# Attention with relative bias, then a leaky-ReLU FFN: one FFN piece fewer per head pair, and the next pair's q and k turned and copied in the pair's first half

## The chip, the cores and the metric

One core of a Trainium2 chip runs the whole program. The metric is the device time of one execution in microseconds (us), median over runs.

## The reference, cut to what matters

```python
# q, k, v: (8, 8, 576, 64), bias_table: (32, 8)
scores = q @ k.T / 8 + bias            # bias depends on the distance of the positions and the head
attn = exp(scores - max); attn /= sum(attn)
x = (attn @ v) as (4608 tokens, 512)   # 8 heads of 64 side by side
h = x @ w_in                           # 512 -> 2048
out = maximum(0.01 * h, h) @ w_out     # 2048 -> 512, float32
```

## The kernel before, in words

The attention goes by pairs of heads: `items` lists 8 batches of 4 pairs, so pair n runs from 0 to 31. The FFN goes by tiles of 512 tokens, nine of them. The engines' orders are the program's own: `manual_schedule` (line 68) keeps on each engine the order in which the code issues, and every engine works its queue in order. What stands where is therefore set by the loop at lines 553 to 596 alone.

For a pair, `qk_mm` (line 296) makes the transposed scores: u = 0 to 3 are the four blocks of 128 keys against queries 0 to 511 (line 311, PSUM tile `ps_s`, two buffers), u = 4 holds the same keys against the last 64 queries (line 304, tile `ps_q`), u = 5 the last 64 keys (lines 314 and 315). `exp` (line 321) takes the exponentials on ScalarE into `at`, and `band` (line 332) multiplies the band around the diagonal with the exponentiated bias on VectorE (line 346). One pair later `av_tails` and `av` (lines 350 and 363) make the value products: a first half for the pair's first head, 20 matmuls at line 370 that VectorE divides at lines 373 and 374 (`rcp`, `opair`), and a second half for the other head. Both halves live in one PSUM tile `ps_o`, which has a single buffer of two banks (tag "o"), and the `ps_q` of the running pair takes the same buffer. `x_transposes` turns the result into `xT`, by TensorE for the first pairs (line 392, copied at line 393) and by a DMA transpose from pair 6 on.

q and k are needed with the head dimension on partitions. `pair_rows` (line 249) packs them (`pr`, line 254), and they are turned on TensorE for pairs 0 to 9 (line 275, six transposes for q and six for k), and by a DMA transpose into `tu` three pairs ahead from pair 10 on (line 262). `transpose_q` and `transpose_k` (lines 286 and 291) then copy them on VectorE into `qt` and `kt`, and line 281 makes a masked copy of the last 64 keys.

The FFN is cut into pieces of four matmuls of 512 columns. An in-piece (line 415, then the leaky ReLU on ScalarE, line 417) makes one block of 128 of the 2048 inner features; four out-pieces (line 426) make 128 tokens of the result, copied on VectorE into `y` (line 431) and stored by SP. Both use the PSUM tag "m" with two buffers. `moe(n)` issues up to n in-pieces, `moe_block` four pieces, two and two, out-pieces if a tile is ready for that and in-pieces otherwise. After pair 31, `moe_rest` issues what is left and may use all PSUM.

In a steady pair before, the queue of TensorE is: scores 0 and 1, tails, first half of the value products of the pair before, in-piece, second half, in-piece, scores 2, 3 and 4, two out-pieces, score 5, two out-pieces, two in-pieces. The copies into `qt` and `kt` for the next pair stand on VectorE behind the last band product and ahead of the copy into `y`. For pairs 5 to 9 (issued in pairs 4 to 8) the twelve transposes stand between score 5 and the second half of the block, both in one "o" tile `ps_tt`.

Of the kernel before, what the change touches and what calls it, by code (L numbers as in the profile page):

```python
# [11 lines left out]
BF16 = mybir.dt.bfloat16  # L12
# [25 lines left out]
def kernel(  # L38
# [17 lines left out]
    P = 128  # L56
    n_pairs = H // 2
# [21 lines left out]
    ps_o_pool = ctx.enter_context(tc.tile_pool(name="ps_o", bufs=1, space=bass.MemoryType.PSUM))  # L79
    ps_m_pool = ctx.enter_context(tc.tile_pool(name="ps_m", bufs=2, space=bass.MemoryType.PSUM))  # L80
# [163 lines left out]
    N = len(items)  # L244
    AHEAD = 3

    prs, turned = {}, {}
# [9 lines left out]
    def by_dma(n):  # L257
        return n >= 2 * n_pairs + 2
# [5 lines left out]
    def turned_pair(n, j):  # L264

        if by_dma(n):
            return turned[n][:, j * NC : (j + 1) * NC, :].rearrange("p c r -> p r c")
        if n <= n_pairs:
            ps = ps_m_pool.tile([P, 8 * P], BF16, name="ps_t", tag="m")
        else:  # L270
            if j == 0:
                turned[n] = ps_o_pool.tile([P, 2, 8 * P], BF16, name="ps_tt", tag="o")
            ps = turned[n][:, j, :]
        for c in range(NC):
            nc.tensor.transpose(ps[:, c * RQ : (c + 1) * RQ], in_=prs[n][0:RQ, j, c, :],
                                identity=ident[0:RQ, 0:RQ])
        return ps[:, 0:S].rearrange("p (c r) -> p r c", c=NC)

    def apart(t):

        nc.vector.tensor_tensor(
            out=t[:, S : S + P].rearrange("p (e i) -> p e i", e=2),
            in0=t[:, NJ * P : S].unsqueeze(1).to_broadcast([P, 2, SL]),
            in1=own, op=ALU.mult)

    def transpose_q(n):
        qt = qts[n] = qt_pool.tile([P, S], BF16, name="qt")
        copy = nc.scalar.copy if n <= n_pairs and n != 1 else nc.vector.tensor_copy
        copy(out=qt[:, 0:S].rearrange("p (r c) -> p r c", c=NC), in_=turned_pair(n, 0))  # L289

    def transpose_k(n):
        kt = kts[n] = kts_[n % 2]
        nc.vector.tensor_copy(out=kt[:, 0:S].rearrange("p (r c) -> p r c", c=NC), in_=turned_pair(n, 1))  # L293
        apart(kt)

    def qk_mm(n, u):

        qt, kt = qts[n], kts[n]
        if u == NJ:
            ps = ps_o_pool.tile([P, 2, 512], FP32, name="ps_q", tag="o")  # L300
            for c in range(NJ):
                for e in range(2):
                    r = slice(e * D, (e + 1) * D)
                    nc.tensor.matmul(ps[:, e, c * SL : (c + 1) * SL], lhsT=kt[r, c * P : (c + 1) * P],
                                     rhs=qt[r, 512:S], start=True, stop=True)
            return ps
        ps = ps_s_pool.tile([P, 2, 512], FP32, name="ps_s")
        if u < NJ:
            for e in range(2):
                r = slice(e * D, (e + 1) * D)  # L310
                nc.tensor.matmul(ps[:, e, :], lhsT=kt[r, u * P : (u + 1) * P], rhs=qt[r, 0:512],  # L311
                                 start=True, stop=True)
        else:
            nc.tensor.matmul(ps[:, 0, :], lhsT=kt[:, S : S + P], rhs=qt[:, 0:512], start=True, stop=True)
            nc.tensor.matmul(ps[:, 1, 0:SL], lhsT=kt[:, S : S + P], rhs=qt[:, 512:S], start=True, stop=True)  # L315
        return ps
# [4 lines left out]
    def exp(n, u, ps):  # L321
        at, at4 = at_view(n), at4_[n % 2]
        if u < NJ:
            nc.scalar.activation(at[:, :, u, 0:512], ps, AF.Exp, scale=scale)  # L324
        elif u == NJ:
            nc.scalar.activation(at[:, :, :, 512:S],  # L326
                                 ps[:, :, 0 : NJ * SL].rearrange("p e (c i) -> p e c i", i=SL),
                                 AF.Exp, scale=scale)
        else:
            nc.scalar.activation(at4[:, 0:S], ps.rearrange("p e i -> p (e i)")[:, 0:S], AF.Exp, scale=scale)  # L330
# [19 lines left out]
    def av_tails(n):  # L350

        b, p = items[n]
        at4 = at4_[n % 2]
        ops_[n] = op_pool.tile([P, NJ + 1, 2 * D], BF16, name="opair")
        ps = outs[n] = ps_o_pool.tile([P, 2, 512], FP32, name="ps_o", tag="o")
        for ic in range(NJ + 1):
            for e in range(2):
                r = slice(e * SL, (e + 1) * SL)
                nc.tensor.matmul(ps[:, e, ic * (D + 1) : (ic + 1) * (D + 1)],  # L359
                                 lhsT=at4[r, ic * P : (ic + 1) * P], rhs=v4[b % NBUF][r, p, :],  # L360
                                 start=(ic == 0), stop=False)
# [15 lines left out]
    def x_by_dma(n):  # L377
        return n_pairs + 2 <= n < N - 1
# [61 lines left out]
    def can(kind):  # L440
        T = made[kind]
        if running[kind] is not None:
            return True
        if kind == "in":
            return T < made["ready"] and T < made["out"] + 2
        return T < made["in"]

    def piece(kind):

        nonlocal share  # L450
        if running[kind] is None:
            running[kind] = (ffn_in if kind == "in" else ffn_out)(made[kind])
            left[kind] = n_fc
            if kind == "in":
                share = left["out"]
        next(running[kind])
        left[kind] -= 1
        if left[kind] == 0:
            next(running[kind], None)
            running[kind] = None  # L460
            made[kind] += 1
# [8 lines left out]
    def moe(n_pieces):  # L470
        for _ in range(n_pieces):
            if can("in"):
                piece("in")

    def moe_block():

        kind = "out" if can("out") else "in"
        for i in range(4):
            if can(kind):
                piece(kind)  # L480
            if i == 1:
                yield
        yield

    def moe_rest():
        rest["on"] = True
        while (kind := choose()):
            piece(kind)

    def finished(n):  # L490
        b, p = items[n]
        if p == n_pairs - 1:
            while made["ready"] < n_tt and (made["ready"] + 1) * TT <= (b + 1) * S:
                made["ready"] += 1
# [17 lines left out]
    def begin(n):  # L512
        b, p = items[n]
        if n == 0:
            load_w_in(0)
            load_v(1, 0, H, False)
            load_w_in(1)
            load_w_out(0)
            load_w_out(1)
        elif 0 < b < B - 1:  # L520
            if p < 2:
                load_qk(b + 1, 4 * p, 4 * p + 4)
            if p > 0:
                load_v_part(b + 1, p - 1)
        if n + 1 < N and not by_dma(n + 1):
            pair_rows(n + 1)
        if n + AHEAD < N and by_dma(n + AHEAD):
            pair_rows(n + AHEAD)
            turn_by_dma(n + AHEAD)
# [22 lines left out]

    for n in range(2, N + 1):
        live = n < N
        early = n + 1 <= n_pairs
        if x_by_dma(n - 2):
            finished(n - 2)
        if live:
            begin(n)
            ps_a, ps_b = qk_mm(n, 0), qk_mm(n, 1)  # L560
            exp(n, 0, ps_a)
            exp(n, 1, ps_b)
        av_tails(n - 1)
        av(n - 1, 0)
        if live:
            band(n, 0)
        if early:
            transpose_q(n + 1)
        moe(1)
        av(n - 1, 1)  # L570
        if live:
            band(n, 1)
        if early:
            transpose_k(n + 1)
        moe(1)
        if live:
            ps_a, ps_b, ps_c = qk_mm(n, 2), qk_mm(n, 3), qk_mm(n, 4)
            exp(n, 2, ps_a)
            band(n, 2)
            exp(n, 3, ps_b)  # L580
            exp(n, 4, ps_c)
            band(n, 4)
        x_transposes(n - 1)
        if not x_by_dma(n - 1):
            finished(n - 1)
        block = moe_block()
        next(block)
        if live:
            ps_a = qk_mm(n, 5)
            exp(n, 5, ps_a)  # L590
            band(n, 5)
        if n + 1 < N and not early:
            transpose_q(n + 1)
            transpose_k(n + 1)
        next(block)
        moe(2)
    moe_rest()


# [28 lines left out]
```

## Time and profile before

| | |
|---|---|
| median of 3 runs | 429.24 us (428.47 to 433.93) |
| profiled execution | 429.74 us, of which the span of its instructions 428.0 us |
| mean granted clock of TensorE | 0.976 |
| busy share of the span | TensorE 88%, ScalarE 56%, VectorE 47%, GpSimd 16% |

A window row gives start and end in us from the span's start and what each engine was busy in it. A timeline row gives start, duration, engine, line, what was written and read, how many instructions were merged, and in brackets how long the engine had stood idle and what ended it. A line "A <- B: total, times, longest" in the view of waits says that A waited for B. A few matmul records are missing from the trace, so counts of matmuls are a little low.

### The profile page before, as it was taken

How to read it: one execution, taken by the hardware profiler on the slowest of the kernel's cores; microseconds unless marked ns; L12 is line 12 of the kernel's file. 1: busy time of each engine (PE TensorE's matmuls, PEld its weight loads, DVE VectorE, ACT ScalarE, POOL GpSimd, SP SyncE). 2: the span in 40 equal slices, each digit the busy share in tenths (PEclk: the TensorE clock that was granted, in tenths of full speed). 3: DMA queues.
4: the chain of work that ended last, by engine and by line, in shares of the span. 5: the costliest groups of instructions: out<-in, count | busy, mean ns of one | idle time of the engine just before them, and what ended most of it. 6: DMA issues, size and time to landing. Idle time of an engine off the chain costs nothing.

```text
span 428.0 us, 8434 instructions
## 1 busy us (share of the span) xinstructions
PE 376.7 (88%) x3458; PEld 191.6 (45%) x3512; DVE 200.2 (47%) x517; ACT 239.5 (56%) x343; POOL 67.8 (16%) x98
## 2 busy tenths in 40 slices
PE   7777688778995999979999999999999999999995
PEld 2454344444443444444444444444444444444442
DVE  5457444665555555555555555555555520010121
ACT  3728475555686666666666666666666626316000
POOL 8734321015002400330042004000000000000000
PEclk9959899999998999999999999999999999999999
DMA  9999993149822984595479536943411100010111
GB/s 106 190 198 193 205 150 57 47 74 163 145 40 47 174 142 66 84 168 98 69 94 177 101 69 91 101 70 69 69 41 41 41 26 25 26 74 0 51 74 74
DMA packets 103613, 39.90 MB, mean 93 GB/s; under 512 B 82576, under 2 KB 97944, under 8 KB 103576
## 3 DMA queue, kind: packets, MB, share of 16 engines
q0 software_dynamic: 53664, 18.36, 41.9%
q1 hardware_dynamic: 49912, 21.02, 23.8%
q8 instruction: 27, 0.44, 0.4%
q14 instruction: 10, 0.08, 0.1%
HBM read 37.68 MB, written 9.45 MB: 110 GB/s over the span
## 4 chain that ended last, share of the span: by engine, by line
PE 55%; DVE 20%; ACT 15%; issue 7%; DMA 1%; another core or an unknown queue 1%; ACTq 0%; POOL 0%; POOLq 0%
PE pm L415 21%; PE pm L426 15%; PE ps_o L370 11%; ACT at L324 8%; DVE at L346 5%; PE ps_s L311 5%; ACT at L330 3%; DVE opair L374 3%; DVE y L431 3%; DVE qt L289 3%; DVE kt L293 3%; ACT at L326 3%; DVE rcp L373 1%; PE ps_o L359 1%; ACT gt L417 1%
## 5 line engine op out<-in xcount | busy, mean ns | idle before, releaser
L415 PE MATMUL pm<-xT,w_in_sb 128*128 128x512 bf16 x546 | 138.4, 379 | 14.8 <-DVE y L431 9.4
L417 ACT ACTIVATE gt<-pm 128x512 bf16<-128x512 f32 x144 | 86.2, 602 | 114.6 <-PE pm L415 114.5
L324 ACT ACTIVATE at<-ps_s 128x1024 bf16<-128x1024 f32 x128 | 124.0, 1027 | 34.0 <-PE ps_s L311 34.0
L426 PE MATMUL pm<-w_out_sb,gt 128*128 128x512 bf16 x553 | 130.7, 380 | 1.9 <-issue 0.7
L346 DVE TENSOR_TENSOR at<-at,hk 128x768 bf16<-128x768 bf16 (+3 forms) x160 | 72.0, 454 | 66.1 <-ACT at L324 30.5
L415 PEld LDWEIGHTS <-w_in_sb 128*128 128x128 bf16 x576 | 52.5, 98 | 71.4 <-issue 19.3
L426 PEld LDWEIGHTS <-gt 128*128 128x128 bf16 x576 | 53.0, 98 | 61.2 <-issue 1.0
L370 PE MATMUL ps_o<-vn,at 128*128 128x65 bf16 x1280 | 52.6, 198 | 5.5 <-DVE opair L374 5.5
L431 DVE COPY y<-pm 128x512 f32<-128x512 f32 x36 | 24.7, 687 | 69.1 <-PE pm L426 66.1
L370 PEld LDWEIGHTS <-at 128*128 128x128 bf16 x1280 | 47.3, 101 | 16.7 <-issue 11.9
L311 PE MATMUL ps_s<-qt,kt 64*128 64x512 bf16 x256 | 41.4, 396 | 10.3 <-DVE kt L293 7.0
L119 POOL DMA_DIRECT2D vn<-in_v_dram x24 | 21.1, 891 | 173.4 <-PE ps_o L370 168.7
L373 DVE RECIPROCAL rcp<-ps_o 128x5 f32<-128x5 f32 x64 | 12.5, 195 | 73.0 <-PE ps_o L370 72.8
L374 DVE TENSOR_TENSOR opair<-ps_o,rcp 128x320 bf16<-128x320 f32 x64 | 31.5, 491 | 2.2
L311 PEld LDWEIGHTS <-kt 64*128 64x128 bf16 x256 | 8.0, 95 | 36.0 <-issue 26.5
L330 ACT ACTIVATE at<-ps_s 128x576 bf16<-128x576 f32 x32 | 21.8, 681 | 1.7 <-PE ps_s L315 1.6
L326 ACT ACTIVATE at<-ps_q 128x512 bf16<-128x512 f32 x32 | 19.7, 617 | 0.0
L359 PEld LDWEIGHTS <-at 64*128 64x128 bf16 x320 | 9.5, 95 | 11.3 <-DVE at L346 2.5
L293 DVE COPY kt<-tu 128x576 bf16<-128x576 bf16 x22 | 14.3, 651 | 0.0
L289 DVE COPY qt<-tu 128x576 bf16<-128x576 bf16 x22 | 14.2, 647 | 0.0
L111 POOL DMA_DIRECT2D qn<-in_q_dram x17 | 12.0, 706 | 12.7 <-DVE pr L254 10.0
L359 PE MATMUL ps_o<-v,at 64*128 64x65 bf16 x320 | 11.1, 193 | 3.0 <-DVE at L346 1.9
(53 smaller groups left out, 165.7 us busy)
## 6 DMA issues: line engine op xcount, KB each, us to landing
out_dram<-y SPq DMA_DIRECT2D x36, 256.0 KB, 2.2
vn<-in_v_dram POOLq DMA_DIRECT2D x28, 128.0 KB, 5.4
qn<-in_q_dram POOLq DMA_DIRECT2D x12, 288.0 KB, 7.2
kn<-in_k_dram POOLq DMA_DIRECT2D x12, 288.0 KB, 7.9
w_in_sb<-in_moe_w_in_dram POOLq DMA_DIRECT2D x2, 1024.0 KB, 14.8
w_out_sb<-in_moe_w_out_dram POOLq DMA_DIRECT2D x2, 1024.0 KB, 16.0
qn<-in_q_dram POOLq DMA_DIRECT2D x4, 144.0 KB, 4.2
kn<-in_k_dram POOLq DMA_DIRECT2D x4, 144.0 KB, 4.5
```

Of the source, the lines that this page charges most:

```text
L293: nc.vector.tensor_copy(out=kt[:, 0:S].rearrange("p (r c) -> p r c", c=NC), in_=turned_pair(n, 1))
L311: nc.tensor.matmul(ps[:, e, :], lhsT=kt[r, u * P : (u + 1) * P], rhs=qt[r, 0:512], start=True, stop=True)
L324: nc.scalar.activation(at[:, :, u, 0:512], ps, AF.Exp, scale=scale)
L326: nc.scalar.activation(at[:, :, :, 512:S], ps[:, :, 0 : NJ * SL].rearrange("p e (c i) -> p e c i", i=SL), AF.Exp, scale=scale)
L330: nc.scalar.activation(at4[:, 0:S], ps.rearrange("p e i -> p (e i)")[:, 0:S], AF.Exp, scale=scale)
L346: nc.vector.tensor_tensor(out=o, in0=o, in1=m, op=ALU.mult)
L370: nc.tensor.matmul(ps[:, ic, :], lhsT=at[:, o : o + P], rhs=vn[b % NBUF][:, c, 2 * p + e, :], start=False, stop=(ic == NJ and c == NJ - 1))
L374: nc.vector.tensor_tensor(out=opair[:, :, e * D : (e + 1) * D], in0=ps[:, :, 0:D], in1=rcp.to_broadcast([P, NJ + 1, D]), op=ALU.mult)
L415: nc.tensor.matmul(pm, lhsT=w_in_sb[:, c, f * P : (f + 1) * P], rhs=xT[c][:, t0 : t0 + TT], start=(c == 0), stop=(c == n_cc - 1))
L417: nc.scalar.activation(gt[:, f, :], pm, AF.Prelu, bias=0.0, scale=1.0, alpha=0.01)
L426: nc.tensor.matmul(pm, lhsT=gt[:, f, ts * P : (ts + 1) * P], rhs=w_out_sb[:, f, :], start=(f == 0), stop=(f == n_fc - 1))
L431: nc.vector.tensor_copy(out=y, in_=pm)
```

## The change

The transposes and copies for the next pair's q and k move up: q's behind the first half of the value products, k's behind the second, in every pair and not in pairs 2 and 3 alone. The transposes on TensorE that used the "o" buffer now use the "m" buffers, one tile for q and one for k. The last `moe(2)` becomes `moe(1)`, so that a full pair holds 28 FFN matmuls in place of 32.

```diff
@@ turned_pair @@
-        if n <= n_pairs:
-            ps = ps_m_pool.tile([P, 8 * P], BF16, name="ps_t", tag="m")
-        else:
-            if j == 0:
-                turned[n] = ps_o_pool.tile([P, 2, 8 * P], BF16, name="ps_tt", tag="o")
-            ps = turned[n][:, j, :]
+        ps = ps_m_pool.tile([P, 8 * P], BF16, name="ps_t", tag="m")
@@ the loop over pairs @@
-        early = n + 1 <= n_pairs
+        more = n + 1 < N
...
-        if early:
+        if more:
             transpose_q(n + 1)
         moe(1)
         av(n - 1, 1)
         if live:
             band(n, 1)
-        if early:
+        if more:
             transpose_k(n + 1)
         moe(1)
...
-        if n + 1 < N and not early:
-            transpose_q(n + 1)
-            transpose_k(n + 1)
         next(block)
-        moe(2)
+        moe(1)
```

The rules that choose pieces are unchanged, but they meet other numbers. FFN matmuls by pair, counted in the two programs (a full pair is two in-pieces in the first half, four out-pieces, and the rest in-pieces; an in-pair has in-pieces alone; the last row holds what follows pair 31):

| pair | 4 | 5 | 6 | 7, 8 | full pairs | in-pairs | short pairs | 31 | from then on |
|---|---|---|---|---|---|---|---|---|---|
| before | 24 | 32 | 24 | 16 each | 32 in 9, 13 to 15, 17 to 30 | 32 in 10 | 16 in 11, 12, 16 | 32 | 8, then 344 |
| after | 20 | 28 | 16 | 16 each | 28 in 9, 10, 13 to 16, 18 to 25, 27 to 30 | 28 in 11, 17, 26 | 12 in 12 | 28 | 8, then 420 |

On VectorE, in a full pair before (line 373 divides the second head; the `at` rows are the bands 1, 2, 4 and 5; then the copies for the next pair, the copy into `y`, and the packing for a pair further on):

```order
L373 RECIPROCAL rcp<-ps_o 128x5
L374 TENSOR_TENSOR opair<-ps_o,rcp 128x5x64
L346 TENSOR_TENSOR at_113<-at_113,hk 128x2x384 x2
L346 TENSOR_TENSOR at_113<-at_113,hk 128x2x320
L346 TENSOR_TENSOR at_0_115<-at_0_115,hk_101 128x192
L289 COPY qt<-tu 128x576
L293 COPY kt_111<-tu 128x576
L281 TENSOR_TENSOR kt_111<-kt_111,own 128x128
L431 COPY y<-pm_2833 128x512
L254 COPY pr<-qn_103 96x768
```

In a full pair after, from the first division on, the `qt` copy stands between the two divisions, the `kt` copy and its masked part behind band 1, and the copy into `y` has only the bands ahead of it:

```order
L369 TENSOR_TENSOR opair<-ps_o,rcp 128x5x64
L341 TENSOR_TENSOR at_114<-at_114,hk 128x2x256
L284 COPY qt<-tu 128x576
L368 RECIPROCAL rcp<-ps_o 128x5
L369 TENSOR_TENSOR opair<-ps_o,rcp 128x5x64
L341 TENSOR_TENSOR at_114<-at_114,hk 128x2x384
L288 COPY kt_110<-tu 128x576
L276 TENSOR_TENSOR kt_110<-kt_110,own 128x128
L341 TENSOR_TENSOR at_114<-at_114,hk 128x2x384
L341 TENSOR_TENSOR at_114<-at_114,hk 128x2x320
L341 TENSOR_TENSOR at_1_116<-at_1_116,hk_101 128x192
L426 COPY y<-pm_2960 128x512
```

So three copies went from behind band 5 to the first half, and `y` moved up by them.

On ScalarE, two full pairs before: the exponentials (lines 324, 326, 330) and the leaky ReLUs of the in-pieces (line 417), which show where TensorE's in-pieces stand:

```order
L324 ACTIVATE at_113<-ps_s 128x2x512 x2
L417 ACTIVATE gt<-pm_2776 128x512
L417 ACTIVATE gt<-pm_2806 128x512
L324 ACTIVATE at_113<-ps_s 128x2x512 x2
L326 ACTIVATE at_113<-ps_q 128x8x64
L330 ACTIVATE at_0_115<-ps_s 128x576
L417 ACTIVATE gt<-pm_2862 128x512
L417 ACTIVATE gt<-pm_2868 128x512
```

One full pair after, lines 319, 321, 325 and 412 being the same four:

```order
L319 ACTIVATE at_114<-ps_s 128x2x512 x2
L412 ACTIVATE gt<-pm_2901 128x512
L412 ACTIVATE gt<-pm_2933 128x512
L319 ACTIVATE at_114<-ps_s 128x2x512 x2
L321 ACTIVATE at_114<-ps_q 128x8x64
L325 ACTIVATE at_1_116<-ps_s 128x576
L412 ACTIVATE gt<-pm_2985 128x512
```

The second in-piece behind the block is gone from the pair; it is issued later, in the end with the 420.

On VectorE in pair 7, where TensorE does the turning, before: both copies read the one tile `ps_tt` behind band 5.

```order
L346 TENSOR_TENSOR at_1_116<-at_1_116,hk_101 128x192 [waits Activation_49]
L289 COPY qt<-ps_tt 128x576 [waits PE_49]
L293 COPY kt_110<-ps_tt 128x576 [waits PE_49]
L281 TENSOR_TENSOR kt_110<-kt_110,own 128x128 [waits DVE_49]
L431 COPY y<-pm_1253 128x512 [waits PE_49]
```

After, each reads a tile of its own, in the first half:

```order
L369 TENSOR_TENSOR opair<-ps_o,rcp 128x5x64 [waits DVE_49]
L341 TENSOR_TENSOR at_114<-at_114,hk 128x2x256 [waits Activation_49]
L284 COPY qt<-ps_t 128x576 [waits PE_49]
L368 RECIPROCAL rcp<-ps_o 128x5 [waits PE_49]
L369 TENSOR_TENSOR opair<-ps_o,rcp 128x5x64 [waits DVE_49]
L341 TENSOR_TENSOR at_114<-at_114,hk 128x2x384 [waits Activation_49]
L288 COPY kt_110<-ps_t 128x576 [waits PE_49]
```

The transposes that fill these tiles moved with them on TensorE, and k's no longer stand behind q's in one tile.

## Rows read from the trace of the kernel before

**Rows 1.** Waits, whole span: who waited for whom, total us, times, longest

```profile
PE pm L415 <- DVE y L431: 9.4, 18, 0.8
...
PE ps_tt L275 <- DVE qt L289: 7.6, 5, 1.7
PE ps_s L311 <- DVE kt L293: 7.0, 3, 3.2
```

**Rows 2.** Windows: length, then PE, PEld, DVE, ACT, POOL busy, clock, DMA, GB/s

```profile
41.11:56.62 15.51, 11.29 (x120) 6.39 (x120) 7.26 (x20) 8.42 (x13) 4.80 (x6) 0.89 1.36 201
56.62:71.05 14.43, 11.05 (x127) 5.91 (x121) 6.03 (x15) 9.26 (x15) 2.68 (x4) 1.00 1.11 79
71.05:81.61 10.56, 9.14 (x109) 5.04 (x105) 5.73 (x14) 6.00 (x10) 0.00 (x0) 1.00 0.31 48
81.61:91.88 10.27, 7.31 (x97) 4.19 (x96) 6.79 (x18) 5.01 (x6) 0.00 (x0) 1.00 0.48 72
...
113.04:124.00 10.96, 10.09 (x110) 5.14 (x104) 5.36 (x14) 9.16 (x16) 0.00 (x0) 1.00 0.23 46
133.66:143.19 9.53, 7.83 (x85) 4.26 (x84) 5.49 (x15) 5.02 (x6) 6.29 (x9) 0.82 1.15 103
175.43:185.12 9.69, 6.43 (x84) 3.42 (x78) 5.04 (x14) 6.86 (x11) 7.03 (x10) 1.00 1.40 113
206.68:217.36 10.68, 10.08 (x110) 5.06 (x103) 5.95 (x15) 6.98 (x12) 0.00 (x0) 1.00 0.45 70
335.49:349.16 13.67, 13.23 (x157) 7.15 (x152) 5.79 (x15) 8.27 (x13) 0.00 (x0) 1.00 0.12 34
349.16:423.44 74.28, 73.95 (x337) 33.56 (x343) 8.52 (x13) 20.30 (x34) 0.00 (x0) 1.00 0.11 43
```

**Rows 3.** Timeline of TensorE in pair 19, a full pair

```profile
206.08 0.61 PE L311 MATMUL ps_s<-qt,kt 64*128 64x512 bf16 x4
...
210.36 0.28 PE L304 MATMUL ps_q<-qt,kt 64*128 64x64 bf16 x8
...
214.28 1.03 PE L415 MATMUL pm<-xT,w_in_sb 128*128 128x512 bf16 x4
215.80 1.02 PE L415 MATMUL pm<-xT,w_in_sb 128*128 128x512 bf16 x4 [0.49 <-DVE y L431]
216.76 0.60 PE L311 MATMUL ps_s<-qt,kt 64*128 64x512 bf16 x4
```

**Rows 4.** Timeline of VectorE in pair 19

```profile
209.16 0.19 DVE L373 RECIPROCAL rcp<-ps_o 128x5 f32<-128x5 f32 x1 [0.53 <-PE ps_o L370]
209.39 0.49 DVE L374 TENSOR_TENSOR opair<-ps_o,rcp 128x320 bf16<-128x320 f32 x1
...
213.69 0.64 DVE L289 COPY qt<-tu 128x576 bf16<-128x576 bf16 x1
214.25 0.64 DVE L293 COPY kt<-tu 128x576 bf16<-128x576 bf16 x1
...
215.07 0.68 DVE L431 COPY y<-pm 128x512 f32<-128x512 f32 x1
```

**Rows 5.** Timeline of TensorE in pair 7, transposes on TensorE

```profile
87.51 0.42 PE L275 MATMUL ps_tt<-ident,pr 96*128 96x96 bf16 x6
89.38 0.42 PE L275 MATMUL ps_tt<-ident,pr 96*128 96x96 bf16 x6 [1.44 <-DVE qt L289]
89.63 1.89 PE L426 MATMUL pm<-w_out_sb,gt 128*128 128x512 bf16 x8
```

**Rows 6.** Timeline of TensorE in pair 5, an in-piece of the block

```profile
63.44 1.02 PE L415 MATMUL pm<-xT,w_in_sb 128*128 128x512 bf16 x3 [1.59 <-ACT gt L417]
```

**Rows 7.** Timeline at the end of pair 16, a short pair

```profile
182.52 0.71 ACT L330 ACTIVATE at<-ps_s 128x576 bf16<-128x576 f32 x1
...
184.69 0.61 PE L311 MATMUL ps_s<-qt,kt 64*128 64x512 bf16 x4 [3.21 <-DVE kt L293]
```

**Rows 8.** Tile tu: time from issue to landing of its DMA transposes

```profile
DMA to landing us min/median/max: 3.3/3.4/10.5
```

## The prediction

> **What bounds the kernel now.** I read the windows by pair first, then the timeline of one full pair on TensorE and on VectorE, then the view of waits. The windows run from the first exponential of a pair to that of the next; in the order shown they are pairs 4, 5, 6, 7, 10, 12, 16, 19 and 31, and the stretch after pair 31 [rows 2]. In pair 19 TensorE is busy 10.08 of 10.68 us, ScalarE 6.98, VectorE 5.95: a full pair is TensorE's. The end is TensorE's alone: 344 FFN matmuls in 74.28 us, so 0.216 us each and a piece of four 0.87 us [rows 2]. Since the number of FFN matmuls is fixed, moving pieces from the pairs to the end gains nothing by itself. What can be gained is time in which TensorE stands.
>
> Where does it stand? In pair 19 the last in-piece starts at 215.80, 1.52 us after the one before it at 214.28, though it has only four matmuls to wait for; 0.49 us of that is shown as idle, ended by the copy into `y` [rows 3]. VectorE explains it: the out-pieces were done when the third piece began, at 214.28, but the `y` copy started at 215.07, behind `qt` (213.69), `kt` (214.25) and the masked copy [rows 4]. The last in-piece needs the PSUM buffer that `y` empties. This comes back 18 times, 9.4 us. Two more waits are of the same family: k's transposes wait for the copy of q's (5 times, 7.6 us), and the first scores of a pair wait for `kt` (3 times, 7.0 us) [rows 1]. Together they are 24.0 us.
>
> **The change part by part.** The sum is made pair by pair, against the profiled execution (429.74 us: span 428.0 and 1.74 outside it). Pairs 0 to 3 don't change, so pair 4 starts at 41.1 [rows 2].
>
> Full pairs, 18 of them after. The last in-piece goes, and with it the wait: from 214.28 TensorE goes on to what stood behind 215.80, so the pair is 10.68 - 1.52 = 9.16 us [rows 3]; 18 make 164.9. Had the piece alone gone, it would be 9.8. The remaining pieces' buffers: the next user of `y`'s buffer is the first in-piece of the next pair, behind scores, tails and the first value products, when `y` is long copied. ScalarE's work falls by one leaky ReLU to some 6.4 us and is not the bound.
>
> The moved copies are not free of danger. `qt` now stands between the two divisions. VectorE idles 0.53 us ahead of the second division, and the copy takes 0.64 [rows 4], so the division comes 0.1 to 0.2 us later. Behind it wait the scores of line 304, which start at 210.36 while the division ends at 209.88 [rows 3, 4]: the slack covers it, and I take 0. If the cover fails, it is 0.2 us in each of 18 pairs, 3.6 us. Below nothing it can hardly be: the other waits of that half stay. `kt` fills the idle stretch ahead of band 2. The copies read `tu` half a pair earlier, but its transposes are issued two pairs before and land in 3.4 us, at worst 10.5 [rows 8], against two pairs of 9. On SP's queue only the stores of `y` come earlier; GpSimd's queue keeps its order.
>
> In-pairs, three after (28 matmuls, none of them out-pieces): pair 10's 10.96 less a piece, 10.1 each, 30.3 in all [rows 2]. Their wait for a leaky ReLU stays.
>
> Pairs 4 to 8, transposes on TensorE. The old block lasts from 87.51 to 89.63, 2.12 us, of which 1.44 is wait [rows 5]; I take it off all five. The transposes themselves, some 0.5 us, now stand in the first half, partly where TensorE waits for the division anyway, and take the two "m" buffers in turn with the pieces. Pair 4: 15.51 - 2.12 - 0.87 = 12.5. Pair 5: 14.43 - 2.12 - 0.87, and 0.9 for transposes and for buffers that are freed by copies further back, 12.3. Pair 6 has eight matmuls fewer (1.73), but in-pieces where it had out-pieces, which wait for ScalarE as pair 5's did, 1.59 us [rows 6]: between 8.8 and the 10.56 of now; I take 9.6, since the last exponential then sits behind a leaky ReLU. Pairs 7 and 8: 10.27 - 2.12 + 0.25 = 8.4 each. Sum 51.2, bounds 48 to 54.
>
> Short pair 12, the one left. Pair 16 shows what such a pair does: the last exponential ends at 183.23 and the next scores start only at 184.69, after 3.21 us of idling for `kt` [rows 7]. With `kt` early, the scores' own buffer, freed by that exponential, is what is late next: 1.4 us of 9.69 go [rows 2]. With one piece fewer I take 8.0, bounds 7.6 and 9.5. The clock in pair 12 of now is 0.82, in the others 1.00 [rows 2], so part of pair 12 ran at 1.2 GHz after standing; up to 1.5 us of that may stay, and is in the upper bound. The Trainium skill (TensorE: Matmul & The Clock Gate, section "Why this matters for your kernels") also warns that a gap in matmuls brings the half clock back; this pair agrees with it, while pair 16 idled as long and kept 1.00.
>
> Pair 31: 13.67 - 0.87 = 12.8 [rows 2]. The end: 420 x 0.216 = 90.7 us. There out-pieces and in-pieces now alternate for two out-groups; the order of buffers leaves at least two pieces between a `y` copy and the next use of its buffer, 1.7 us against 0.68 [rows 4], so I add nothing; if each were exposed, 2 us. Last, 4.56 us from the last matmul to the span's end stay.
>
> Sum: 41.1 + 51.2 + 164.9 + 30.3 + 8.0 + 12.8 + 90.7 + 4.6 = 403.6 us of span, 405.3 with what lies outside. The profiled execution is 0.5 above the median of the three runs, so I predict 405. The gain of 24.4 is the 24.0 of the three waits, which is the check on the sum.
>
> **The rivals.** First, the bubble moves. The buffers of tag "m" stay two, and the transposes now draw on them as well. If the copy into `y` still ends a wait in each full pair, say ahead of the next pair's first in-piece, the 9.4 us [rows 1] come back: 414.5. For it: what ended the wait was the release of a buffer of that tag [rows 3]. Against it: in rows 4 the lateness is that of three copies ahead of `y`, not of too few buffers. The Trainium skill (Perfetto Trace Analysis, section "Optimization Strategy") says that a gap repeating on the engine that should be saturated can mean too little PSUM for the next tile. By that rule the change cures nothing, and the time is this rival's.
>
> Second, another chain sets a floor to the pair. Pairs with half the FFN work still took 9.53 and 9.69 us [rows 2]. If 9.7 is the floor of exponentials, bands and divisions, the 18 full pairs lose 18 x 0.54 = 9.7, and the time is 415. Against it: those pairs ended in the wait for `kt` [rows 7], which goes.
>
> Third, slower. The q copy holds up VectorE's second division, line 304's scores wait for the PSUM buffer that it frees, and everything behind them on TensorE waits too. If this takes back all that the full pairs and in-pairs gave up, they stay at 10.68 and 10.96 while the longer end comes on top, and only pairs 4 to 8 and 12 keep their gain: 405.3 + 18 x 1.52 + 3 x 0.87 = 435.3, 435 as a median. It needs the division 1.5 us later; from 24.4 / 21 = 1.2 us in each of these pairs on the kernel is slower than before. The idle 0.53 in rows 4 leaves it 0.1 to 0.2.
>
> Fourth, faster: pairs 5 and 6 lose ScalarE's wait as well and pair 12 shrinks to 7.6: 401. That the change doesn't do what it says is excluded by the order of the built program.
>
> **How the numbers follow.** My forecast has 0.76, with its own range 401 to 410: full pairs 9.1 to 9.36 each (minus 1 to plus 3.6 us), early pairs plus or minus 3, pair 12 up to 1.5 more, the end up to 2 more, not all at once. The bubble has 0.08, the floor 0.08, slower 0.03, faster than forecast 0.05. The range 400 to 414 leaves out most of the two rivals near 415 and the slow one. A measurement of this kernel can tell about 2% from no change, so faster means under 420.7 and slower over 437.8. All cases but the third are faster; the third lies at the edge of no change, or over 437.8 if the early pairs lose too: faster 0.95, within 2% 0.04, slower 0.01.
>
> **What would show it.** Right: the wait of in-pieces for `y` and that of k's transposes for `qt` are gone; full pairs take 9.1 to 9.3 us at a clock of 1.00; the stretch behind pair 31 takes some 91 us for 420 matmuls. Wrong: in-pieces waiting for `y` in the first half (first rival); full pairs at 9.6 or more with TensorE waiting for an exponential or a band (second); line 304's scores waiting for a division (third). Early pairs much over 54 us in sum would say that the "m" buffers are too few for transposes and pieces together.

## The result, and the profile after

The changed kernel takes 403.95 us (median of 4 runs, 402.57 to 403.97); the kernel before took 431.18 in its 4 runs beside it. The ratio is 0.936, 95% interval 0.929 to 0.944: faster by 6.4%. The profiled execution took 403.95 us, its span 402.2, at a mean granted clock of 0.983.

The page of the changed kernel, busy time by engine:

```profile
PE 372.2 (93%) x3460; PEld 191.0 (47%) x3512; DVE 201.0 (50%) x517; ACT 238.4 (59%) x343; POOL 69.0 (17%) x98
```

TensorE is now busy 93% of the span, 88% before. The next view lists what TensorE waited for, whole span: total us, times, longest.

```profile
PE pm L410 <- ACT gt L412: 5.3, 5, 1.5
PE ps_s L306 <- ACT at L325: 3.6, 5, 1.1
```

The three waits of [rows 1], 24.0 us together, are no longer in this list. Two others grew, the in-pieces' wait for a leaky ReLU and the scores' wait for the exponential of u = 5 (line 325, before 330). In the kernel before the same view has for them:

```profile
PE pm L415 <- ACT gt L417: 2.4, 2, 1.6
...
PE ps_s L311 <- ACT at L330: 1.8, 3, 0.6
```

The windows by pair, from first exponential to first exponential as in [rows 2]; pairs 4 to 8, 11, 12, 13, 19, 31, and what follows:

```profile
41.38:53.23 11.85, 9.30 (x116) 5.15 (x116) 6.95 (x20) 7.80 (x13) 2.64 (x3) 1.00 1.26 206
53.23:65.07 11.84, 10.12 (x123) 5.61 (x117) 5.94 (x15) 8.73 (x14) 4.80 (x7) 1.00 1.64 142
65.07:74.61 9.54, 7.33 (x99) 4.25 (x94) 5.14 (x12) 6.97 (x11) 0.00 (x0) 1.00 0.47 65
74.61:82.92 8.31, 7.47 (x97) 4.22 (x99) 6.48 (x18) 5.03 (x7) 0.00 (x0) 1.00 0.46 57
82.92:91.13 8.21, 7.17 (x97) 4.11 (x96) 6.53 (x18) 5.02 (x7) 5.11 (x7) 1.00 1.12 126
...
109.65:119.74 10.09, 9.22 (x106) 4.74 (x100) 5.33 (x14) 8.56 (x15) 0.00 (x0) 1.00 0.35 77
119.74:126.88 7.14, 5.67 (x79) 3.01 (x72) 4.56 (x11) 6.20 (x10) 4.47 (x6) 1.00 0.81 90
126.88:136.66 9.78, 9.50 (x107) 4.96 (x107) 6.87 (x18) 6.55 (x10) 3.38 (x5) 1.00 1.76 116
183.44:192.60 9.16, 9.11 (x107) 4.67 (x99) 6.02 (x15) 6.38 (x11) 0.00 (x0) 1.00 0.36 81
294.42:307.20 12.78, 12.39 (x156) 6.81 (x151) 5.83 (x15) 7.68 (x12) 0.00 (x0) 1.00 0.18 55
307.20:397.83 90.63, 90.21 (x411) 40.93 (x419) 9.85 (x15) 26.88 (x45) 0.00 (x0) 1.00 0.11 41
```

In pair 19 TensorE is busy 9.11 of 9.16 us: almost no idle time is left in a full pair. The timeline of VectorE in the next full pair shows the new order that answers to [rows 4]:

```profile
194.47 0.65 DVE L284 COPY qt<-tu 128x576 bf16<-128x576 bf16 x1
...
195.33 0.49 DVE L369 TENSOR_TENSOR opair<-ps_o,rcp 128x320 bf16<-128x320 f32 x1
...
196.21 0.65 DVE L288 COPY kt<-tu 128x576 bf16<-128x576 bf16 x1
...
200.42 0.69 DVE L426 COPY y<-pm 128x512 f32<-128x512 f32 x1 [0.71 <-PE pm L421]
```

The `y` copy, which stood behind three others, now waits for the last out-piece itself. The same pair on TensorE, to be held against [rows 3]:

```profile
192.00 0.61 PE L306 MATMUL ps_s<-qt,kt 64*128 64x512 bf16 x4
...
196.29 0.28 PE L299 MATMUL ps_q<-qt,kt 64*128 64x64 bf16 x8
...
200.22 1.03 PE L410 MATMUL pm<-xT,w_in_sb 128*128 128x512 bf16 x4
201.18 0.61 PE L306 MATMUL ps_s<-qt,kt 64*128 64x512 bf16 x4
```

From scores to scores it is 9.18 us, and no row of this view, shown or left out, has a bracket: TensorE does not stand in this pair.

### The profile page after: what moved, and what is told of

Its sections match the earlier page's. It is cut to its first block, busy times and chain, and to the rows that moved or that the text cites. A ratio compares the mean times of both kernels' runs of the same rounds, so it can differ in the third digit from the quotient of the medians.

```text
span 402.2 us, 8433 instructions
## 1 busy us (share of the span) xinstructions
PE 372.2 (93%) x3460; PEld 191.0 (47%) x3512; DVE 201.0 (50%) x517; ACT 238.4 (59%) x343; POOL 69.0 (17%) x98
## 4 chain that ended last, share of the span: by engine, by line
PE 80%; DVE 8%; ACT 6%; issue 3%; another core or an unknown queue 1%; ACTq 0%
PE pm L421 30%; PE pm L410 26%; PE ps_o L365 11%; PE ps_s L306 7%; ACT at L319 4%; DVE opair L369 2%; DVE at L341 2%; PE ps_w L495 2%; PE ps_o L354 1%; PE ps_s L309 1%; ACT at L321 1%; DVE rcp L368 1%; PE ps_q L299 1%; DVE qt L284 1%; ACT gt L412 1%
## 5 line engine op out<-in xcount | busy, mean ns | idle before, releaser
L119 POOL DMA_DIRECT2D vn<-in_v_dram x24 | 22.2, 932 | 146.4 <-PE ps_o L365 140.1
L368 DVE RECIPROCAL rcp<-ps_o 128x5 f32<-128x5 f32 x64 | 12.4, 194 | 41.2 <-PE ps_o L365 41.1
```

The source lines that it names most:

```text
L119: nc.gpsimd.dma_start(out=vn[i][:, c, :, 0:D], in_=v[b, :, c * P : (c + 1) * P, :].rearrange("h s d -> s h d"),)
```

## The experiments

The theory: the gain is three waits on TensorE, and all three come from where the copies stand on VectorE (experiment 6 shows that this is not so for the transposes of pairs 4 to 8). The rivals: the removed piece brings the gain; two "m" buffers are too few; another chain sets a floor to the pair; and the copy ahead of the second division costs something. During these runs the kernel before took 431.76 us (first four experiments) and 432.42 (last four).

**1. Early copies, the fourth in-piece kept.** Edit to the changed kernel:

```diff
         next(block)
-        moe(1)
+        moe(2)
```

> The q and k copies and transposes stand early as in the changed kernel, but a full pair keeps 32 FFN matmuls. Theory (the copies ahead of y were the cause of the wait, and the number of pieces only shifts work): the copy into y is done 0.7 us behind the out-pieces, before the second in-piece wants its buffer, so the wait of in-pieces for y is gone, a full pair takes 9.17 + 0.87 = 10.04 us, 344 matmuls stay for the end, and the time is about 403, within 1% of the changed kernel. Rival (taking the last in-piece out is what removed the wait): 18 waits of about 0.5 us stay and the time is about 413 to 415.

Measured: 403.88 us, ratio 0.936 (0.932 to 0.940), the same as with the piece removed. The window of a full pair, then the end of a full pair on TensorE:

```profile
188.28:198.39 10.11, 10.11 (x112) 5.06 (x104) 6.02 (x15) 6.98 (x12) 0.00 (x0) 1.00 0.49 74
```

```profile
185.78 1.97 PE L410 MATMUL pm<-xT,w_in_sb 128*128 128x512 bf16 x8
187.68 0.61 PE L306 MATMUL ps_s<-qt,kt 64*128 64x512 bf16 x4
```

The last two in-pieces run back to back, eight matmuls in 1.97 us, though the tag has two buffers as before. A full pair costs 0.95 us more than with 28 matmuls, and in return 76 matmuls (420 less 344) need not be done at the end. So the early copies alone bring the whole gain, and removing the piece on top of them moves work and saves nothing that can be measured.

**2. The piece removed, copies left late.** Edit to the kernel before:

```diff
         next(block)
-        moe(2)
+        moe(1)
```

> Only the in-piece is taken out of the pair (28 FFN matmuls); copies and transposes stay late. Theory: no in-piece is left to wait for y, and the copy of k ends just when the remaining in-piece does, so full pairs still come down to about 9.2 us; the waits of k's transposes for q's copy stay (5 times, 7 to 8 us) and so do those of the first scores for kt in short pairs; about 416. Rival (the early copies are what shortens full pairs): with late copies the scores of the next pair wait for kt in every pair, by about what y cost, and the time is 425 or more.

Measured: 421.48 us, ratio 0.977 (0.973 to 0.981), 5.5 us more than I expected. Windows of pairs 4 to 7 and of one full pair, then two rows of TensorE's timeline in pair 5:

```profile
40.57:55.85 15.28, 11.56 (x117) 6.67 (x116) 7.33 (x20) 7.82 (x12) 4.76 (x6) 0.78 1.29 204
55.85:72.12 16.27, 12.99 (x125) 6.25 (x117) 6.03 (x15) 8.66 (x14) 2.67 (x4) 0.79 1.32 100
72.12:84.28 12.16, 8.03 (x103) 4.53 (x97) 5.94 (x15) 6.97 (x12) 0.00 (x0) 0.89 0.11 17
84.28:96.95 12.67, 10.41 (x98) 5.63 (x96) 6.09 (x16) 5.02 (x7) 0.00 (x0) 0.70 0.19 38
...
201.39:210.55 9.16, 9.16 (x108) 4.67 (x98) 5.96 (x16) 6.38 (x10) 0.00 (x0) 1.00 0.35 81
```

```profile
65.89 0.64 PE L275 MATMUL ps_tt<-ident,pr 96*128 96x96 bf16 x6 [1.69 <-DVE qt L289]
66.32 5.27 PE L415 MATMUL pm<-xT,w_in_sb 128*128 128x512 bf16 x12
```

In full pairs the missing piece removes the wait as well as the early copies do (9.16 us): nobody needs `y`'s buffer before the next pair. But the transposes still wait for q's copy, and there the clock falls: behind the stand shown, twelve matmuls take 5.27 us, 0.44 each, twice the 0.216 of the end of the kernel before [rows 2], that is at 1.2 GHz in place of 2.4. With 10.29 for pair 8, pairs 4 to 8 take 66.7 us, 5.6 more than the 61.1 before, though they hold 16 FFN matmuls less; that is the miss of 5.5.

**3. Copies late, but `y` copied ahead of them.** In the kernel before, from pair 9 on:

```diff
-        if n + 1 < N and not early:
+        if n + 1 < N and not early and not by_dma(n + 1):
             transpose_q(n + 1)
             transpose_k(n + 1)
         next(block)
+        if n + 1 < N and by_dma(n + 1):
+            transpose_q(n + 1)
+            transpose_k(n + 1)
         moe(2)
```

> The kernel before with one swap on VectorE, from pair 9 on: the copy into y stands ahead of the copies into qt and kt, nothing else moves. Theory (order on VectorE): the wait for y goes, but kt is now 0.7 us later and the next scores wait some 0.3 us for it; full pairs about 10.35, time about 424. Rival (too few PSUM buffers of tag m): in-pieces still wait for y 18 times, the time is 430 or more.

Measured: 426.48 us, ratio 0.989 (0.985 to 0.993): a gain of 1.1%, below the 2% from which a version counts as faster, and 2.5 us more than I expected. VectorE at the end of pair 19, and TensorE there:

```profile
217.25 0.69 DVE L431 COPY y<-pm 128x512 f32<-128x512 f32 x1 [0.71 <-PE pm L426]
...
218.41 0.65 DVE L293 COPY kt<-tu 128x576 bf16<-128x576 bf16 x1
```

```profile
217.05 1.97 PE L415 MATMUL pm<-xT,w_in_sb 128*128 128x512 bf16 x8
219.11 0.11 PEld L311 LDWEIGHTS <-kt 64*128 64x128 bf16 x4 [0.59 <-DVE kt L293]
219.12 0.60 PE L311 MATMUL ps_s<-qt,kt 64*128 64x512 bf16 x4
```

With `y` first, the last two in-pieces run back to back, with two buffers and 32 matmuls: the rival of too few buffers falls. What is gained there is partly lost to the next pair's scores: TensorE's weight loads for them (PEld) now wait 0.59 us for `kt`, and pair 19 takes 10.27 us, 10.68 before and 10.11 in experiment 1. Pairs 12, 13 and 17 became longer, 11.71, 11.81 and 11.65 us at clocks of 0.75, 0.86 and 0.87, where they took 9.53 at 0.82, 10.87 and 10.87 at 1.00; this takes back 3.9 us. With `y` and the copies both at the end of a pair of 32 matmuls, one of them is late. Moving the copies to the first half frees both (experiment 1), and so does taking the piece out (experiment 2).

**4. The second division held up.** In the changed kernel, for the pairs whose q comes by DMA, a second copy of the turned q into a tile that nobody reads:

```diff
             transpose_q(n + 1)
+            if by_dma(n + 1):
+                nc.vector.tensor_copy(out=spare[:, 0:S].rearrange("p (r c) -> p r c", c=NC),
+                                      in_=turned_pair(n + 1, 0))
         moe(1)
```

> The changed kernel with a second, useless copy of the turned q on VectorE (0.65 us) right behind the copy into qt, in pairs 9 to 30; the output is unaffected. It measures the slack of the third rival of the prediction. From the trace the second division ends 0.26 us before the load for line 299's scores, so 0.65 us more should show as a wait of 0.4 us in each of 22 pairs: full pairs about 9.6 us, time about 413. If the slack were ample: 404. If the copy's delay came through in full: 418.

Measured: 405.61 us, ratio 0.940 (0.936 to 0.943), 1.7 more than the changed kernel and 7 less than I expected. One full pair, TensorE and VectorE together:

```profile
192.31 0.60 PE L307 MATMUL ps_s<-qt,kt 64*128 64x512 bf16 x4
...
196.14 0.49 DVE L370 TENSOR_TENSOR opair<-ps_o,rcp 128x320 bf16<-128x320 f32 x1
196.68 0.17 PEld L300 LDWEIGHTS <-kt 64*128 64x128 bf16 x8 [0.41 <-DVE opair L370]
196.69 0.29 PE L300 MATMUL ps_q<-qt,kt 64*128 64x64 bf16 x8
```

The division ends 4.32 us after the pair's first scores, against 3.82 in the changed kernel (195.82 - 192.00); the scores of line 300 start at 4.38 against 4.29. So half a microsecond of lateness costs 0.09 per pair: the changed kernel still has some 0.4 us of slack here.

**5. No in-piece behind the block, 24 matmuls in a full pair.** In the changed kernel:

```diff
         next(block)
-        moe(1)
```

> The changed kernel with one in-piece fewer still: 24 FFN matmuls in a full pair, 496 behind pair 31. Theory (TensorE has no wait left in full pairs, so pieces only change places): full pairs 9.17 - 0.96 = 8.2 us, in-pairs 9.2, no short pair any more, six in-pairs instead of three; sum about 403, within 1% of the changed kernel. Rival (a chain of exponentials, bands and divisions sets a floor near 9 us): full pairs stay at 9 or more, the 76 matmuls at the end cost 16 us and the time is 415 or more.

Measured: 403.15 us, ratio 0.933 (0.928 to 0.938), again the same time. A full pair, and TensorE's longest wait:

```profile
191.87:200.18 8.31, 8.31 (x94) 4.30 (x92) 6.21 (x16) 5.99 (x9) 2.25 (x4) 1.00 1.51 169
```

```profile
PE pm L410 <- ACT gt L412: 7.6, 8, 1.5
```

No other chain holds a pair at 9.7, nor at 9: TensorE is busy through all of 8.31 us. That rival falls. What stays are in-pieces that wait for a leaky ReLU, in the pairs without out-pieces.

**6. Early copies only where TensorE does the turning (pairs 4 to 8), 32 matmuls.** In the changed kernel:

```diff
-        more = n + 1 < N
+        more = n + 1 < N and not by_dma(n + 1)
...
+        if n + 1 < N and not more:
+            transpose_q(n + 1)
+            transpose_k(n + 1)
         next(block)
-        moe(1)
+        moe(2)
```

> Only pairs 2 to 8, whose next q and k are turned on TensorE, get the early transposes and copies and the m buffers; from pair 9 on copies stay late, and all full pairs keep 32 FFN matmuls. It prices that part alone. Theory: pairs 4 to 8 take 50 to 51 us as in the first run with early copies instead of 61, full pairs stay at 10.7 with 18 waits for y; time about 420 to 421. Rival (the part of the early pairs is small, the gain is all in full pairs): 426 or more.

Measured: 422.03 us, ratio 0.973 (0.968 to 0.979). Two of the three waits are back nearly as they were:

```profile
PE pm L410 <- DVE y L426: 9.2, 18, 0.7
PE ps_s L306 <- DVE kt L288: 6.9, 3, 3.2
```

Pairs 4 to 8 take 51.0 us, 10.1 less than before. By the medians the whole kernel gains 10.4 us, but by the profiled executions 6.8 (429.74 to 422.93): pairs 12 and 17 take 11.70 us at a clock of 0.63 and 12.04 at 0.89, where they took 9.53 at 0.82 and 10.87 at 1.00. The step from here to experiment 1, the early copies from pair 9 on, is 18 us, of which these two waits are 16.

In pairs 4 to 8 the edit does three things at once: it moves the transposes and copies, gives q and k a tile each, and takes the tiles from the "m" buffers. No run separates them, but the trace shows that VectorE's order is not what ended this wait. The changed kernel's pair 7, to be held against [rows 5]:

```profile
75.86 0.42 PE L270 MATMUL ps_t<-ident,pr 96*128 96x96 bf16 x6
...
77.03 0.75 DVE L284 COPY qt<-ps_t 128x576 bf16<-128x576 bf16 x1
...
77.44 0.42 PE L270 MATMUL ps_t<-ident,pr 96*128 96x96 bf16 x6
```

The copy of q starts 0.75 us after q's transposes end, in pair 8 1.01, and before it was 0.51 to 0.88: it comes no sooner. But TensorE now has the second half of the value products between the two groups of transposes, and in pairs 4, 7 and 8 k's transposes begin some 0.33 us before the copy of q ends, as here (77.44 against 77.78), where in the one tile of the kernel before they waited for its end.

**7 and 8. The exponential of u = 4 and its band behind the first half of the block, where the block is in-pieces.** In such pairs ScalarE worked the exponentials of u = 2, 3 and 4 ahead of the leaky ReLUs that empty the two "m" buffers. Experiment 7 has the 24 matmuls of experiment 5, experiment 8 the 28 of the changed kernel:

```diff
-            exp(n, 4, ps_c)
-            band(n, 4)
+            behind = not can("out")
+            if not behind:
+                exp(n, 4, ps_c)
+                band(n, 4)
...
         next(block)
         if live:
+            if behind:
+                exp(n, 4, ps_c)
+                band(n, 4)
```

> As the one with 24 matmuls, and in pairs whose block is made of in-pieces the exponential of line 321 and its band stand behind the first two in-pieces instead of ahead of them, so that their leaky ReLUs come 0.6 us earlier on ScalarE. Theory: the waits of in-pieces for a leaky ReLU (1.5 us in early pairs, 0.8 in in-pairs, nine pairs) fall by 0.4 to 0.6 us each, and it is 3 to 5 us faster than the same without it: 398 to 400. Rival (the delayed exponential is waited for instead): no gain.

> The changed kernel (28 matmuls) with the same swap on ScalarE in pairs whose block is made of in-pieces: six pairs. Theory: 0.4 to 0.6 us each, 2.4 to 3.6 in all, about 400.5 to 401.5. Rival (the delayed exponential is waited for instead): 404 or more.

Measured, 7: 397.1 us (6 runs, 396.35 to 399.05), ratio 0.919 (0.915 to 0.922), the best of all versions and 0.9 under the range that I expected. 8: 401.68 us, ratio 0.929 (0.925 to 0.933). The wait in 7, and its in-piece in pair 11, which had stood 0.76 us in experiment 5:

```profile
PE pm L410 <- ACT gt L412: 1.6, 6, 0.3
```

```profile
108.81 1.89 PE L410 MATMUL pm<-xT,w_in_sb 128*128 128x512 bf16 x8 [0.27 <-ACT gt L412]
```

The wait goes from 7.6 us in experiment 5 to 1.6, and the time by 6.05. In 8 it goes from 5.3 to 1.3, but the time by 2.3 alone, and by the profiled executions 1.5 (403.95 to 402.49). The windows of pairs 12 and 13 of 8, and the timeline of TensorE in pair 13, show the largest part of the rest:

```profile
117.17:124.32 7.15, 5.72 (x80) 3.02 (x73) 4.41 (x11) 6.21 (x11) 4.48 (x6) 1.00 0.85 96
124.32:135.60 11.28, 11.07 (x108) 5.82 (x107) 7.02 (x19) 6.55 (x11) 3.50 (x5) 0.85 1.58 108
```

```profile
124.53 0.39 PE L306 MATMUL ps_s<-qt,kt 64*128 64x512 bf16 x2 [1.13 <-ACT at L325]
...
125.75 1.90 PE L410 MATMUL pm<-xT,w_in_sb 128*128 128x512 bf16 x4
```

Pair 13 takes 11.28 us at a clock of 0.85 in 8, and 9.78 at 1.00 in the changed kernel, behind the same wait of 1.13 us: 1.5 us lost. This need not be so in every execution of 8: the profiled one has a mean clock of 0.979, and the three at 0.983 took 401.52 to 401.68 us. Experiment 7 has no short pair, and its clock stayed at 1.00 in every pair from 3 on.

## Why the prediction was right

The forecast was 405 with a gain of three waits, and the span came out by nearly the terms named: pair 4 starts at 41.38 (forecast 41.1); pairs 4 to 8 take 49.75 (51.2); the 18 full pairs 9.35, 9.78 and sixteen of 9.16 to 9.18, 165.9 in all (164.9); the three in-pairs 30.3 (30.3); pair 12 7.14 (8.0); pair 31 12.78 (12.8); from there to the span's end 95.0 (95.3). The sum is 402.2 against 403.6; the forecast was too high in pairs 4 to 8 and in pair 12, by 1.45 and 0.86 us, and too low in the full pairs, by 1.0, so the errors partly cancel.

- **Full pairs, 9.16.** Right, and for a reason that the prediction only half gave. It took the piece and its wait off together; experiments 1 and 2 show that the wait goes by either edit alone. Its "Had the piece alone gone, it would be 9.8" was wrong: in experiment 2 such a pair takes 9.16. That moving pieces gains nothing by itself, as the prediction's first part said, holds once the copies are early, with 32, 28 and 24 matmuls: 403.88, 403.95 and 403.15 us. With late copies it does not, since the moved piece takes the wait along.
- **The q copy ahead of the second division.** The prediction allowed 0.1 to 0.2 us of lateness inside the slack. In the trace the division ends 3.82 us after the pair's first scores, 3.80 before ([rows 3, 4], 209.88 - 206.08): the copy fits into the wait for the value products. Experiment 4 then sized the slack that is left at some 0.4 us. The slower rival needed 1.5 us.
- **Pairs 4 to 8.** 1.45 us less than forecast, within its bounds: pairs 4 and 5 gave 0.65 and 0.46 of it. Pair 4's clock is 1.00, where it was 0.89 [rows 2]; the forecast had kept that loss. The prediction counted the wait of k's transposes as "of the same family" as that for `y`; the rows of experiment 6 show that it went by what stands between the transposes on TensorE and by the tiles of their own, not by a sooner copy.
- **Pair 12.** The mechanism was right, and its place was off by one pair. Line 325's exponential, which frees the scores' buffer, is next in line; it lengthens not pair 12 (7.14) but pair 13, whose second pair of scores waits 1.13 us for it: 9.78 in place of 9.16. Both together take 16.92 us, forecast 17.16. The row:

```profile
127.10 0.39 PE L306 MATMUL ps_s<-qt,kt 64*128 64x512 bf16 x2 [1.13 <-ACT at L325]
```

- **In-pairs.** "Their wait for a leaky ReLU stays" held, and so did the wait of pairs 5 and 6, 1.51 us in each, which the fourth rival would have taken away. Experiment 7 then took most of both. In pair 11, TensorE's row is:

```profile
116.46 2.75 PE L410 MATMUL pm<-xT,w_in_sb 128*128 128x512 bf16 x11 [0.77 <-ACT gt L412]
```

- **First rival, too few buffers.** Refuted by experiments 1 and 3. The Trainium skill's rule (Perfetto Trace Analysis, section "Optimization Strategy") that a repeating gap can mean too little PSUM did not hold for this gap: two buffers were enough once the engine that empties them had nothing else ahead.
- **Second rival, a floor of 9.7.** Refuted by experiment 5, with full pairs of 8.31 us.
- **What each part of the change is worth.** Early turning in pairs 4 to 8 about 10 us (the windows of experiment 6), early copies from pair 9 on about 18 more (experiment 1 against 6, with the clock that 6 lost in pairs 12 and 17), the removed piece nothing on top of them, though 10 us without them (experiment 2).

The sum of the three waits is 24.0 us and the two profiled executions differ by 25.8. The wait for line 325 and that for leaky ReLUs grew by 4.7 us together, so the three waits alone do not make the gain. That the forecast gain of 24.4 met their 24.0 so closely was luck as a check. What the two traces show is 21.3 us less idle time on TensorE (51.3 to 30.0 us of the span) and 4.5 us less busy time (376.7 to 372.2) for the same work, with a few records missing in both. Of the 4.5, pairs 4 and 12 are 2.4 by their windows, beyond the piece of 0.87 that left each; there the clock was 0.89 and 0.82 before and is 1.00 now. I did not run these two pairs apart.

## What to carry to other kernels

Where the busiest engine stands for a buffer, look at what the engine that empties it has in its queue ahead of that, and at how early the input of each of those instructions was there: in a full pair three copies whose inputs had long landed stood ahead of the one that was needed. When the total of the bound engine's work is fixed, count a gain in its waits and its clock, and distrust the shorter pair: with early copies 32, 28 and 24 matmuls per pair gave one time. A stretch that is made shorter while its waits stay can become longer by the clock, as pairs 5 and 6 of experiment 2 did (16.27 and 12.16 us, 14.43 and 10.56 before), so both are to be read after such a change.

## What the runs showed of the hardware

Which stand costs the clock was not to be foreseen from its length. In pair 5 of the kernel before TensorE stood 1.59 us [rows 6] and then 1.69, and its clock stayed at 1.00 through the pair [rows 2]; its timeline:

```profile
66.65 0.42 PE L275 MATMUL ps_tt<-ident,pr 96*128 96x96 bf16 x6 [1.69 <-DVE qt L289]
66.90 3.62 PE L415 MATMUL pm<-xT,w_in_sb 128*128 128x512 bf16 x16
```

Sixteen matmuls take 3.62 us there. In experiment 2 the same pair stood 1.69 us for the same copy, and the twelve matmuls behind it took 5.27. A wait of 1.13 us in pair 13 left 1.00 in the changed kernel and 0.85 in experiment 8. The Trainium skill (TensorE: Matmul & The Clock Gate, section "Why this matters for your kernels") warns that long idle gaps between bursts of matmuls bring the half clock back. The stands named here are all shorter than those that it speaks of; after two of them the clock fell all the same, and after others of the same length it did not. What told them apart was not tried and stays open.
